# TensorE's branch around the rare paths, placed behind a product that waits for VectorE's last scaling

## The chip, the cores and the metric

The kernel runs on one core of a Trainium2 chip. The metric is the device time of one execution in microseconds (us). The kernel before takes 631.93 us, the median of three executions (631.75, 631.93 and 632.38).

## The reference, cut to what matters

Two branches over the same 2048 x 448 input are mixed with a gate for each token:

```
g = sigmoid((x * gate_w).sum(-1))
a = Cr @ (x @ Wr.T) - Ci @ (x @ Wi.T)            # Fourier mixing, real part
gates = softmax(x @ wg); top 2 of 8 experts, weights cw renormalised
h = gelu(einsum("nd,edf->nef", x, w1))            # 8 experts, 448 -> 1792
b = einsum("ne,ned->nd", cw, einsum("nef,efd->ned", h, w2))
return g * a + (1 - g) * b
```

The change touches none of these results.

## The kernel before, in words

The program has one straight part and one conditional part. The straight part computes the Fourier branch by the symmetries of the DFT matrices and the experts with a fixed capacity of rows for each (496 to 576). The conditional part, the rare paths, repeats work in a general way: tokens beyond an expert's capacity, and inputs whose DFT matrices lack the symmetries. VectorE finds out in the straight part whether either is needed and writes it into a small tile, `flags`. With these inputs neither is needed.

The expert work runs over `jobs`, pairs of an expert and one of its 14 blocks of 128 hidden columns. `up` makes a block's hidden values (the matmuls of line 777), `down` multiplies them by the second weight matrix (line 837) into one accumulator for each tile of up to 128 rows. The last four blocks of the last expert are multiplied together, in `down(*range(last - 3, last + 1))`, tile after tile. When a tile's products are complete, `combine` scales it by the tokens' weights (VectorE in lines 881 and 888, ScalarE in line 890), and `scatter` has GpSimd send its rows to `out` by an indirect DMA (line 900). The very last tile, 112 rows, is the one scaling of line 881; the rows that it adds to were fetched before (line 896), and its scatter is the last work of the straight part.

Then come two lines that all five engines execute:

```
    rest = nc.values_load(flags[0:1, 2:3], min_val=0, max_val=1)
    ctx.enter_context(tc.If(rest > 0))
```

Each engine loads the flag into a register (TENSOR_LOAD, line 1127), compares, and takes a branch over the code of the rare paths (COMPARE_BRANCH, shown under `_compat.py:109`) to the end of the program. There it sets right the semaphores that the skipped code would have changed (EVENT_SEMAPHORE, `_compat.py:109`), and all engines meet (line 1322): SyncE waits for the semaphores of every engine and of every DMA queue one after the other, each engine reports, and GpSimd clears the semaphores.

Each engine has its own sequence of instructions, written out in the order of the program (`tc.manual_schedule` for TensorE, VectorE, ScalarE and SyncE). TensorE's ends with the matmuls of line 837; nothing in its sequence waits for the scaling that follows them, so its TENSOR_LOAD and its branch stand directly behind its last matmul. The rows of an engine's sequencer are marked by a q (PEldq for TensorE's, DVEq, ACTq, POOLq, SPq). The engines' instructions themselves are brought from memory by DMAs, the rows of kind "instruction" among the DMA queues: q8 moves 16 KB a packet and q14 8 KB.

Of the kernel before, what the change touches and what calls it, by code (L numbers as in the profile page):

```python
# [9 lines left out]
F32 = mybir.dt.float32  # L10
# [9 lines left out]
P = 128  # L20
# [47 lines left out]
def tiles_of(cap):  # L68
    return [min(P, cap - c * P) for c in range((cap + P - 1) // P)]
# [3 lines left out]
def tile_kernel(ctx: ExitStack, tc: tile.TileContext, xt, xrows, xplain, wg, whid, cq, cw, cspec, edge, refs, wquad, whall, cgen, wcat, out):  # L73
    nc = tc.nc
    te, ve, se, gp, sp = nc.tensor, nc.vector, nc.scalar, nc.gpsimd, nc.sync

    keep = ctx.enter_context(tc.tile_pool(name="keep", bufs=1))
    rp = ctx.enter_context(tc.tile_pool(name="rp", bufs=1))
    stream = ctx.enter_context(tc.tile_pool(name="stream", bufs=3))
    ps = ctx.enter_context(tc.tile_pool(name="ps", bufs=3, space=bass.MemoryType.PSUM))  # L80
# [130 lines left out]
    def apart(e):  # L211
        return CAPS[e] - FULL * P == Q
# [601 lines left out]
    def down(*us, behind=None):  # L814
        e = jobs[us[0]][0]
        tl = tiles_of(CAPS[e])
        if jobs[us[0]][1] == 0:
            for c in range(len(tl)):
                Y[c] = psy.tile([P, 512], F32, name=f"y{BANKS[c]}")
        sent = []  # L820
        turns = [(c, u) for c in range(len(tl)) for u in us]
        if len(us) == 4:
            turns[3:5] = turns[4:2:-1]
        for c, u in turns:
            f, n = jobs[u][1], tl[c]
            if c == FULL and apart(e):
                few(e, u, sent)
                continue
            m = n if c < FULL else 2 * n
            cs = slice(c * P, c * P + m)  # L830
            wh, wl = (w[:, :D] for w in V[u])
            gh, gl = GH[u]
            steps = [(gh[:, cs], wh), (gh[:, cs], wl)]
            if c < FULL:
                steps.append((gl[:, cs], wh))
            for s, (a, b) in enumerate(steps):
                te.matmul(Y[c][:m, :D], a, b, start=f == 0 and s == 0, stop=f == NF - 1 and s == len(steps) - 1)  # L837
            if f == NF - 1:
                combine(e, c, n, sent)
                if behind and c == FULL - 2:  # L840
                    behind()
        for u in us:
            del W[u], V[u], GH[u]

    def few(e, u, sent):
        f = jobs[u][1]
        if f + 1 not in LOTS:
            return
        lot = range(u - f + max(b for b in LOTS if b <= f), u + 1)
        for i in range(0, len(lot), NQ):  # L850
            group = lot[i : i + NQ]
            wide = NQ // len(group)
            for j in range(NQ):
                v = group[j // wide]
                cs = slice(j % wide * (D // wide), (j % wide + 1) * (D // wide))
                te.matmul(Y[FULL][j * Q : (j + 1) * Q, cs], REST[v], RAW[v][1][:, cs], start=f < LOTS[1] and i == 0, stop=f == NF - 1 and i + NQ >= len(lot), tile_position=(0, j * Q))
        for v in lot:
            del RAW[v], REST[v]
        if f == NF - 1:
            rt["rear"] = Y[FULL], sent  # L860
# [16 lines left out]
    def combine(e, c, n, sent):  # L877
        wt = rt["wgt"][:n, e, c : c + 1]
        ys = mp.tile([P, D], F32, name="ys", bufs=NCT)
        if (e, c) == (E - 1, FULL - 1):  # L880
            ve.scalar_tensor_tensor(ys[:n], Y[c][:n, :D], wt, rt["base"][:n], op0=OP.mult, op1=OP.add)
        elif c == FULL:
            yt = mp.tile([P, D], F32, name="yt", bufs=1)
            ve.tensor_copy(yt[:n], Y[c][n : 2 * n, :D])
            ve.tensor_tensor(yt[:n], Y[c][:n, :D], yt[:n], OP.add)
            ve.tensor_scalar(ys[:n], yt[:n], wt, None, op0=OP.mult)
        elif c % 2 == 0:
            ve.tensor_scalar(ys[:n], Y[c][:n, :D], wt, None, op0=OP.mult)  # L888
        else:
            se.activation(ys[:n], Y[c][:n, :D], AF.Copy, scale=wt)  # L890
        scatter(e, c, n, ys, sent, None if (e, c) == (E - 1, FULL - 1) else OP.add)
# [177 lines left out]
    def side_work(s):  # L1069
        s -= SIDE  # L1070
        quad_dma(*divmod(s - 2, PACE))
        if s == 3:
            edges_dma()
        if s == 6:
            edges()
        q, r = divmod(s - 4, PACE)
        if 0 <= q < len(units):
            quad_check(q, r)
        e, f = divmod(s + SIDE, NF)
        if e > 1 and apart(e - 1) and f < 2:  # L1080
            rear(e - 1, f)
        if 1 <= e <= NQT and f in (2, NF - 1):
            blend(2 * (e - 1) + f // (NF - 1))
        if e == NQT + 1 and f == 3:
            blend_mid()
        end = 4 + PACE * len(units)
        if s == end:
            verdict()
        if s == end + 1:
            tell()  # L1090
        if len(summed) > len(mixed):
            send(*summed[len(mixed)])
            if len(mixed) == NT:
                tc.keep_in_program_order(gp.drain())
                ahead(E - 1, FULL - 1)
        if s > end + 1 and 1 <= f < (NF - 3 if e == E - 1 else NF - 1) and len(summed) < NT:
            mix(len(summed))

    up(UP, lambda: advance(2))
    for u in range(UP, last):  # L1100
# [19 lines left out]
        if not split:  # L1120
            side_work(u - UP)
    down(*range(last - 3, last + 1))
    order.close()
    late.close()

# [7 lines left out]
    with tc.For_i(0, n_ov) as j:  # L1133
# [31 lines left out]
        for f in range(NF):  # L1165
# [3 lines left out]
            acc = ps.tile([P, 512], F32, name="acc")  # L1169
# [18 lines left out]
    with tc.For_i(0, n_a) as j:  # L1188
# [3 lines left out]
        for h in range(2):  # L1192
            hf = full.tile([P, 2 * D], F32, name="hf")
            for u in range(2):
                acc = ps.tile([P, 512], F32, name="acc")
# [4 lines left out]
    with tc.For_i(0, n_b) as i:  # L1200
        acc = psy.tile([P, 512], F32, name="y0")
# [125 lines left out]
```

## Time and profile before

| | |
|---|---|
| median of three executions | 631.93 us |
| the profiled execution, its whole time | 632.4 us |
| its span, first to last instruction | 630.8 us |
| VectorE, ScalarE, GpSimd busy | 80%, 46%, 35% of the span |
| moved by DMA | 122.96 MB |
| instruction fetches on q8, on q14 | 30 and 33 packets |

The whole time is 1.6 us above the span. TensorE is in work through nearly all of the span; its granted clock is 0.998 of full speed. What the change touches lies in the last 8 us, where the engines finish one after the other, so the views to read are the instructions in order of time near the end, the rows of single source lines (they hold the sequencers' own instructions, which count as no engine's busy time), and the DMA queues in short windows. In the views of windows and of DMA queues a packet counts with its whole time where it starts.

### The profile page before, as it was taken

What the parts mean: (1) busy time and instruction counts of PE and PEld (TensorE: products, weight loads), DVE (VectorE), ACT (ScalarE), POOL (GpSimd) and SP (SyncE); (2) the same over time, 40 slices, a digit from 0 to 9 for tenths busy, and PEclk for the clock granted to TensorE, in tenths of its full rate; (3) what the DMA queues carried; (4) which work ended last, traced back from release to release, by engine and by line L of the source; (5) the groups of instructions that cost most, each with busy time, mean ns of one, the idle gap of its engine ahead of it and who ended that gap; (6) DMA issues with size and microseconds to landing.
All of it is one profiled execution on the core that took longest, in us unless ns stands there. A gap on an engine that the chain in (4) does not pass through costs nothing. (4 is left out here: it accounts for less than half of the span.)

```text
span 630.8 us, 10868 instructions
## 1 busy us (share of the span) xinstructions
PE 621.8 (99%) x3581; PEld 556.5 (88%) x3581; DVE 503.8 (80%) x1261; ACT 287.1 (46%) x588; POOL 217.7 (35%) x199
## 2 busy tenths in 40 slices
PE   9999999999999999999999999999999999999995
PEld 5999999989998999989999788888888888888884
DVE  7889797689977999779896799988997788666551
ACT  2543233365565565564664434333342334544440
POOL 2210084554254353344440444333241342142113
PEclk9999999999999999999999999999999999999999
DMA  8546454588777777786776867879566737768734
GB/s 344 181 158 212 163 178 140 162 184 289 227 235 193 203 241 230 226 192 205 245 233 218 196 189 240 259 200 286 177 219 193 153 120 150 157 156 162 154 70 60
DMA packets 58751, 122.96 MB, mean 195 GB/s; under 512 B 8305, under 2 KB 31921, under 8 KB 58689
## 3 DMA queue, kind: packets, MB, share of 16 engines
q1 hardware_dynamic: 47376, 101.95, 49.6%
q0 software_dynamic: 11168, 20.20, 17.9%
q8 instruction: 30, 0.49, 0.3%
q14 instruction: 33, 0.26, 0.1%
q10 hardware_dynamic: 144, 0.07, 0.0%
HBM read 106.09 MB, written 16.08 MB: 194 GB/s over the span
## 5 line engine op out<-in xcount | busy, mean ns | idle before, releaser
L777 PE MATMUL acc<-X,hi 128*128 128x288 f32 (+3 forms) x1050 | 216.5, 342 | 0.0
L667 POOL DMA_INDIRECT xg<-xrows,piece x115 | 127.5, 1109 | 208.3 <-DVE xq L676 132.0
L777 PEld LDWEIGHTS acc<-X,hi 128*128 128x128 f32 x1050 | 173.6, 188 | 19.5 <-issue 1.1
L837 PE MATMUL y<-dn,gh 128*128 128x448 f32 (+1 forms) x458 | 167.5, 366 | 0.0
L837 PE MATMUL y<-up,gh 128*128 128x448 f32 (+1 forms) x458 | 167.3, 365 | 0.0
L837 PE MATMUL y<-up,gl 128*128 128x448 f32 (+1 forms) x444 | 162.5, 366 | 0.0
L784 ACT ACTIVATE g<-acc 128x288 f32<-128x288 f32 (+3 forms) x126 | 61.4, 489 | 189.1 <-issue 117.6
L777 PE MATMUL acc<-X,lo 128*128 128x288 f32 (+3 forms) x672 | 134.6, 322 | 0.0
L777 PEld LDWEIGHTS acc<-X,lo 128*128 128x128 f32 x672 | 105.4, 188 | 10.3
L900 POOL DMA_INDIRECT out<-ys,tok x36 | 65.6, 1822 | 111.6 <-DVE ys L888 53.2
L837 PEld LDWEIGHTS y<-up,gh 128*128 128x128 f32 (+1 forms) x458 | 85.8, 187 | 7.6
L837 PEld LDWEIGHTS y<-dn,gh 128*128 128x128 f32 (+1 forms) x458 | 85.8, 187 | 7.3
L801 DVE TENSOR_TENSOR gl<-g,gh 128x512 fp32r<-128x512 f32 (+1 forms) x111 | 76.5, 689 | 18.5 <-ACT gh L795 11.0
L941 DVE CUSTOM_DVE_ANT_0 junk<-quads 128x512 f32<-128x512 f32 x128 | 88.0, 688 | 2.6 <-issue 0.3
L837 PEld LDWEIGHTS y<-up,gl 128*128 128x128 f32 (+1 forms) x444 | 83.2, 187 | 7.7 <-DVE gl L801 0.9
L223 DVE TENSOR_TENSOR lo<-raw,hi 128x512 fp32r<-128x512 f32 x112 | 77.1, 688 | 2.6 <-ACT hi L218 1.1
L797 DVE CAST gh<-g 128x512 fp32r<-128x512 f32 (+2 forms) x69 | 30.3, 439 | 54.8 <-ACT g L784 53.4
L218 ACT ACTIVATE hi<-raw 128x512 fp32r<-128x512 f32 x112 | 69.5, 620 | 0.0
L223 DVE TENSOR_TENSOR dn<-row,up 128x448 fp32r<-128x448 f32 x112 | 69.2, 618 | 0.0
L218 ACT ACTIVATE up<-row 128x448 fp32r<-128x448 f32 x112 | 63.3, 565 | 0.0
L784 ACT ACTIVATE g<-g 128x256 f32<-128x256 f32 x42 | 17.6, 418 | 46.3 <-DVE g L783 37.1
L782 ACT ACTIVATE g<-acc 128x256 f32<-128x256 f32 x42 | 15.9, 379 | 43.2 <-PE acc L777 31.7
(276 smaller groups left out, 433.4 us busy)
## 6 DMA issues: line engine op xcount, KB each, us to landing
quads<-cq SPq DMA_DIRECT2D x64, 512.0 KB
raw<-wcat SPq DMA_DIRECT2D x112, 256.0 KB
row<-wcat SPq DMA_DIRECT2D x112, 224.0 KB
out<-yt SPq DMA_DIRECT2D x21, 224.0 KB
xraw<-xt SPq DMA_DIRECT2D x8, 512.0 KB
out<-ot POOLq DMA_DIRECT2D x16, 224.0 KB
cw<-cw SPq DMA_DIRECT2D x4, 512.0 KB
xg<-xrows,piece POOLq DMA_INDIRECT x115
```

Of the source, the lines that this page charges most:

```text
L218: se.activation(hi[:, : raw.shape[-1]], raw, AF.Copy)
L223: ve.tensor_tensor(lo[:, :n], raw, r32(hi[:, :n]), OP.subtract)
L667: st = gp.indirect_dma_start(out=xg[:, q], out_offset=None, in_=xrows, in_offset=bass.IndirectOffsetOnAxis(ap=rt["piece"][:, e, g : g + 1] ...
L777: te.matmul(acc[:, :m], a, b, start=s == 0, stop=s == len(steps) - 1)
L782: se.activation(g[:, cs], acc[:, n : 2 * n], AF.Copy)
L784: se.activation(g[:, cs], g[:, cs] if both else acc[:, :n], AF.Gelu_apprx_tanh)
L797: ve.tensor_copy(gh[:, :top], g[:, :top])
L801: ve.tensor_tensor(gl[:, :main], g[:, :main], r32(gh[:, :main]), OP.subtract)
L837: te.matmul(Y[c][:m, :D], a, b, start=f == 0 and s == 0, stop=f == NF - 1 and s == len(steps) - 1)
L900: st = gp.indirect_dma_start(out=out, out_offset=bass.IndirectOffsetOnAxis(ap=rt["tok"][:n, e, c : c + 1], axis=0), in_=ys[:n], in_offset= ...
L941: ve.tensor_tensor_reduce(out=junk[:, :512], in0=row(a[0])[:, a[1] * 512 : a[1] * 512 + 512], in1=row(b[0])[:, b[1] * 512 : b[1] * 512 + 5 ...
```

## The change

Ahead of the flag's load, one value for each partition is set to zero by VectorE, and TensorE multiplies that column with itself into one element of an accumulator that nobody reads:

```diff
     down(*range(last - 3, last + 1))
+    done = keep.tile([P, 1], F32, name="done")
+    ve.memset(done, 0.0)
+    te.matmul(ps.tile([P, 512], F32, name="acc")[:1, :1], done, done, start=True, stop=True)
     order.close()
     late.close()
```

On VectorE the memset stands between the last scaling (line 881) and the flag's load:

```order
 L888 TENSOR_SCALAR ys<-y_6883,wgt 128x448
 L881 SCALAR_TENSOR_TENSOR ys<-y_6884,wgt,yt 112x448
-L1127 TENSOR_LOAD flags
+L1124 MEMSET done 128x1
+L1130 TENSOR_LOAD flags
 _compat.py:109 COMPARE_AND_BRANCH
```

The memset has no wait of its own; it follows the scaling in VectorE's order.

On TensorE, at the end of the straight part (y_6884 is the last tile's accumulator), the new product stands between the last matmul and the flag's load:

```order
 L837 MATMUL y_6884<-dn,hi 112x448
 L837 MATMUL y_6884<-up,lo 112x448
-L1127 TENSOR_LOAD flags
+L1125 MATMUL acc<-done 1x1
+L1130 TENSOR_LOAD flags
 _compat.py:109 COMPARE_AND_BRANCH
```

The product waits for a semaphore of VectorE, which the memset raises. The flag's load and the branch, which directly followed the last matmul, now follow the product. The sequences of ScalarE, GpSimd and SyncE are the same but for line numbers, three higher behind the change (1127 is 1130, 1322 is 1325).

`done` takes 4 bytes of each partition in the pool `keep`. Pools begin at multiples of 32 bytes, so those that are laid out behind `keep` from the same side (`rp`, `stream` with the weights, `hid`, `lp`, `xp` with the experts' inputs) begin 32 bytes later; the other pools stay where they were.

## The prediction

> **What bounds the kernel now.** I read the page first: who is busy through the span.
>
> ```profile
> span 630.8 us, 10868 instructions
> PE 621.8 (99%) x3581; PEld 556.5 (88%) x3581; DVE 503.8 (80%) x1261; ACT 287.1 (46%) x588; POOL 217.7 (35%) x199
> ```
>
> TensorE is in work for 621.8 of 630.8 us, and the change adds to its stream nothing before its last regular matmul. So only the tail can move. The second view is the instructions in order of time (start, duration) at the end.
>
> ```profile
> 618.43 0.64 ACT L890 ACTIVATE ys<-y,wgt 128x448 f32<-128x448 f32 x1 [4.23 <-PE y L837]
> ...
> 622.86 0.36 PE L837 MATMUL y<-up,lo 128*112 128x448 f32 x1
> 623.26 0.69 DVE L881 SCALAR_TENSOR_TENSOR ys<-y,wgt,yt 112x448 f32<-112x448 f32 x1 [1.72 <-PE y L837]
> 624.22 0.96 POOL L900 DMA_INDIRECT out<-ys,tok  x1 [0.85 <-DVE ys L881]
> ```
>
> Last matmul to 623.2, last scaling to 623.95, last scatter issued by 625.2; then 5.6 us in which no engine computes. What fills them stands in the sequencers' rows (duration in ns min/median/max, first and last start in us): the flag's loads of line 1127, the branches of `_compat.py:109`, the meeting of line 1322, and SyncE's waits.
>
> ```profile
> L1127 ACTq TENSOR_LOAD <-flags x1: 468/468/468, 618.4 to 618.4; - x1
> L1127 PEldq TENSOR_LOAD <-flags x1: 835/835/835, 619.5 to 619.5; - x1
> L1127 DVEq TENSOR_LOAD <-flags x1: 544/544/544, 623.3 to 623.3; - x1
> L1127 POOLq TENSOR_LOAD <-flags x1: 918/918/918, 624.0 to 624.0; - x1
> ```
>
> ```profile
> _compat.py:109 ACTq COMPARE_BRANCH x1: 45/45/45, 619.0 to 619.0; - x1
> _compat.py:109 PEldq COMPARE_BRANCH x1: 4982/4982/4982, 620.4 to 620.4; - x1
> _compat.py:109 DVEq COMPARE_BRANCH x1: 72/72/72, 623.9 to 623.9; - x1
> _compat.py:109 POOLq COMPARE_BRANCH x1: 57/57/57, 625.0 to 625.0; - x1
> ```
>
> ```profile
> L1322 SPq EVENT_SEMAPHORE x14: 17/28/28, 629.2 to 630.7; - x14
> ...
> L1322 SPq DRAIN x3: 7/7/13, 629.9 to 630.2; - x3
> ...
> L1322 PEldq DRAIN x2: 8/8/8, 625.7 to 630.3; - x2
> ```
>
> ```profile
> SPq L1322 <- DMA out<-ys,tok: 26.8, 1, 26.8
> ```
>
> The end hangs on the last scatter: SyncE waits for its landing until 629.2, and the fixed meeting takes the other 630.8 - 629.2 = 1.6 us. TensorE's branch is the odd row: 4.98 us (620.4 to 625.4) where the others need 0.05 to 0.07. It is off the path now: TensorE has reported at 625.7.
>
> Why does the scatter, issued by 625.2, land only at 629.2? The third view is the DMA queues in short windows (packets, MB, share of 16 engines' time). For 622.0 to 622.2, then for 621.9 to 624.2:
>
> ```profile
> q8 instruction: 1, 0.02, 60.7%
> ```
>
> ```profile
> q8 instruction: 1, 0.02, 5.3%
> ```
>
> One 16 KB fetch starts at about 622.1, 1.7 us into TensorE's branch, and takes 0.053 x 16 x 2.3 = 1.95 us, to 624.05; the branch ends 1.35 us later. So the branch waits for code. For 626.5 to 626.65, 626.5 to 631.0, and for 627.0 to 629.0 with its 40 slices of 0.05 us:
>
> ```profile
> q8 instruction: 1, 0.02, 59.8%
> ```
>
> ```profile
> q8 instruction: 1, 0.02, 2.0%
> ```
>
> ```profile
> DMA  0000000000000000000700000000000100000000
> ...
> q0 software_dynamic: 3, 0.01, 2.1%
> ```
>
> A second fetch starts at about 626.58, 1.2 us after the branch ended, and takes 0.020 x 16 x 4.5 = 1.44 us, to 628.0. Between 627 and 629 just three packets of the scatters start (q0), the first in the slice 627.95 to 628.0, as that fetch ends, the last two by 628.6. All others had started before 627.0:
>
> ```profile
> 626.00:626.50 0.50, 0.00 (x0) 0.00 (x0) 0.00 (x0) 0.00 (x0) 0.00 (x0) 1.00 0.72 215
> 626.50:627.00 0.50, 0.00 (x0) 0.00 (x0) 0.00 (x0) 0.00 (x0) 0.00 (x0) 1.00 0.44 132
> 627.00:627.50 0.50, 0.00 (x0) 0.00 (x0) 0.00 (x0) 0.00 (x0) 0.00 (x0) 1.00 0.00 0
> ```
>
> (The two numbers at a row's end are DMA share and GB/s.) I read: one of the 16 DMA engines held the end of the last scatter behind TensorE's second fetch. The last packet starts near 628.57 and the scatter has landed at 629.2, 0.6 us later. Without that fetch it would have landed at 627.3 to 627.6.
>
> **The change, part by part.**
>
> *The memset.* The same form elsewhere:
>
> ```profile
> L205 DVE MEMSET raw<- x2: 59/59/59, 37.9 to 37.9; 128x1 f32 x2
> ```
>
> 0.06 us behind the scaling's end at 623.95: 624.0. It delays VectorE's own flag load and branch by as much, and VectorE is done some 5 us before the end: nothing.
>
> *The product.* TensorE is idle from 623.2, so its work costs nothing. Its wait is the change: queued behind it on TensorE are the flag's load, the branch, and the two fetches. All move from 619.5 to 624.1 (GpSimd's flag load, released by the same scaling, starts at 624.0; its DMA at 624.22; so 624.0 to 624.2). No DMA of the kernel is moved and no queue passed.
>
> *The flag's load.* 0.835 us is TensorE's own; bounds 0.47 and 0.92 (ScalarE's, GpSimd's). The branch follows 0.1 us later (620.4 less 620.3). Branch start: 624.1 + 0.84 + 0.1 = 625.0 (624.6 to 625.2), instead of 620.4.
>
> *The branch.* At most 4.98 us as now. Below: request 1.2 (second fetch), transfer 1.0, tail 0.6 (as the scatter's landing) = 2.8. The transfer is the mean over all q8 packets, 0.003 x 16 x 630.8 / 30:
>
> ```profile
> q8 instruction: 30, 0.49, 0.3%
> ```
>
> I take request 1.4, between its two values; transfer 1.4, that of the second fetch, which met the same scatter; tail 1.0, between 0.6 and 1.35. Sum 3.8: the branch ends at 628.8 (627.4 to 630.2).
>
> *The end through TensorE.* Its reports follow 0.3 us behind the branch (625.4 to 625.7). SyncE passes its waits one after the other (14 rows), and which of them are TensorE's the row does not tell. From there to the end it is between 0.9 us (SyncE's drain at 629.9 to 630.8) and 1.6 us (the whole meeting); I take 1.2. Span by this path: 628.8 + 0.3 + 1.2 = **630.3** (628.6 to 631.7).
>
> *The end through the scatter.* The fetch that stood at 622.1 would start near 625.0 + 1.4 = 626.4, while the scatter still runs (share 0.72 and 0.44), and the second fetch would follow only behind the branch, after the landing. So the scatter meets one fetch again, or just misses it. Landing between 627.3 and 629.2; half of a 1.4 us transfer lost gives 628.2. Span: 628.2 + 1.6 = 629.8 (628.9 to 630.8).
>
> *The 32 bytes* by which weights and inputs move cost nothing that I can find. The nearest rows are two differences of line pairs 1047 and 1049, whose sources start one element apart and which take the same time:
>
> ```profile
> 600.82 0.39 DVE L1047 TENSOR_TENSOR ot<-fold 128x225 f32<-128x225 f32 x1
> 601.13 0.39 DVE L1049 TENSOR_TENSOR ot<-fold 128x224 f32<-128x224 f32 x1
> ```
>
> They speak for VectorE alone. For TensorE and the loads nothing is shown; 0.2% either way stays open.
>
> *Sum.* The later path is TensorE's: span 630.3, with the 632.4 - 630.8 = 1.6 us around it 631.9, which is 0.5 below the profiled execution's own 632.4. That execution is the highest of three, 0.45 over the median, and whether its excess lies in this tail cannot be told. If it does, the tail of the median execution has no 0.5 to give; if not, the time would be 631.4. I take the middle: **631.7**.
>
> **Where a page speaks against it.** On ScalarE the flag's load starts at 618.4, with the scaling of 618.43 that waited 4.23 us for TensorE; on VectorE at 623.3, with the scaling of 623.26. In both, what stands behind a waiting instruction waits too. On TensorE the load started at 619.5, 3.4 us ahead of the last matmul's start, so its sequencer runs far ahead of the array; but those matmuls waited for nothing. [...]
>
> **The rivals.**
>
> 1. *The branch does not move.* TensorE queues the waiting product and goes on to the branch at 620.4. Then both fetches stay and the time is that of now: 632.4 against the profiled execution, 631.9 against the median. For it: the 3.4 us lead. Against: the two engines' rows. 0.10.
>
> 2. *Both fetches miss the scatter and the branch is short.* The fetch starts at 626.7 or later, behind the scatter's last packets, or slips through; landing at 627.5, and a branch at its lower bounds ends by 627.6. Span 629.0 to 629.1, time 630.6, and 630.2 to 630.6 on the median's scale: faster by 0.2 to 0.3%. For it: with the first fetch gone from 622.1, no DMA engine starts the last scatter late. Against: the fetch is due at 626.2 to 626.9, the scatter's packets start until 627.0, and the branch would have to lose 2.2 of its 5 us. 0.15.
>
> 3. *The branch becomes the end, at full length: slower.* All of its 4.98 us is its own and not the traffic's. From 625.2 it ends at 630.2, and the span is 630.2 + 0.3 + 1.2 = 631.7, time 633.3: 0.9 over the profiled execution, 0.2% over the median. It decides from the point where the branch ends after 629.0, as then TensorE's report passes the landing of 629.2 less the waits ahead of it. For it: only one such branch is measured. Against: its fetch ran beside three scatters, and a mean fetch takes half of 1.95 us. 0.07, and 0.01 more that the 32 bytes cost time.
>
> **How the numbers follow.** Forecast 0.67, the three rivals 0.33 (0.10, 0.15, 0.08). About 0.2%, 1.26 us, is what a measurement of this kernel can tell from no change: below 630.67 is faster, above 633.19 slower. The forecast's own spread (630.7 to 632.9) lies inside, and so does rival 1: same 0.77. Faster 0.15, rival 2. Slower 0.08. The range reaches from rival 2's middle, 630.4, to 632.9, a little short of rival 3.
>
> **What would show it.** Right: TensorE's flag load starts at 624.0 to 624.2; its branch starts near 625.0 and lasts 3 to 4.5 us; no q8 packet starts between 614 and 626; SyncE's wait for the scatter ends before 629.0, and a wait for TensorE may take its place. Wrong: TensorE's load still at 619.5 (rival 1); a landing before 627.6 with a branch of under 3 us (rival 2); a branch of 5 us with the landing well before it (rival 3). A matmul or a load of weights that is longer by a constant share through the whole span would mean that the 32 bytes count, and that the tail was the wrong place to look.

## The result, and the profile after

The changed kernel takes 638.58 us (median of five, 638.05 to 638.78) against 631.87 us before (631.55 to 632.38): a ratio of 1.0104, 95% interval 1.0089 to 1.0119. It is slower by 6.7 us, and its time lies far above the predicted range, which ended at 632.9.

The tail did about what was forecast. In order of time, at the end of the changed kernel:

```profile
628.79 0.37 PE L837 MATMUL y<-up,lo 128*112 128x448 f32 x1
629.20 0.68 DVE L881 SCALAR_TENSOR_TENSOR ys<-y,wgt,yt 112x448 f32<-112x448 f32 x1 [1.76 <-PE y L837]
629.83 0.06 DVE L1124 MEMSET done<- 128x1 f32 x1
629.96 0.09 PEld L1125 LDWEIGHTS acc<-done 128*1 128x1 f32 x2 [1.19 <-DVE done L1124]
629.96 0.19 PE L1125 MATMUL acc<-done 128*1 128x1 f32 x2 [0.80 <-DVE done L1124]
630.16 0.96 POOL L900 DMA_INDIRECT out<-ys,tok  x1 [0.89 <-DVE done L1124]
```

TensorE's flag load and branch, SyncE's final meeting and its wait, in the rows of their source lines and of SyncE's waits:

```profile
L1130 PEldq TENSOR_LOAD <-flags x1: 826/826/826, 630.0 to 630.0; - x1
```

```profile
_compat.py:109 PEldq COMPARE_BRANCH  x1: 4418/4418/4418, 630.9 to 630.9; - x1
```

```profile
L1325 SPq EVENT_SEMAPHORE  x14: 17/28/28, 635.3 to 636.8; - x14
```

```profile
SPq L1325 <- DMA out<-ys,tok: 27.0, 1, 27.0
```

And the DMA queues from 631.9 to 634.0, then from 633.2 to 636.0 (with its 40 slices of 0.07 us) and from 635.5 to 637.0:

```profile
q0 software_dynamic: 56, 0.16, 24.3%
q8 instruction: 1, 0.02, 5.5%
```

```profile
DMA  0000000000500000002000000000000000000000
...
q0 software_dynamic: 4, 0.01, 2.0%
```

```profile
q8 instruction: 1, 0.02, 4.0%
```

The load waits for the product and the branch moves with it. The branch's fetch now falls on the last scatter. It takes 0.055 x 16 x 2.1 = 1.85 us, by its record in the trace from 632.09 to 633.93. The scatter's last four packets start only from 633.9 on, as the fetch ends. The second fetch comes behind the landing. SyncE waits for the scatter until 635.3. From the last matmul's start to the end of the span it was 630.8 - 622.86 = 7.94 us; now it is 636.9 - 628.79 = 8.11 us. The tail has cost 0.2 us. The other 5.9 us of the 6.1 by which these two profiled executions differ had been lost before the last matmul started.

Two long stretches show where. Before, from 140 to 340 us and from 360 to 560 us (busy us and count of instructions for each engine; the first pair is TensorE's matmuls):

```profile
140.00:340.00 200.00, 200.00 (x1232) 184.03 (x1231) 175.37 (x455) 117.30 (x255) 79.82 (x60) 1.00 0.75 227
360.00:560.00 200.00, 200.00 (x933) 174.54 (x932) 168.32 (x406) 79.49 (x148) 64.53 (x57) 1.00 0.68 192
```

After:

```profile
140.00:340.00 200.00, 200.00 (x1221) 182.52 (x1220) 173.05 (x448) 117.44 (x251) 77.22 (x60) 1.00 0.73 219
360.00:560.00 200.00, 200.00 (x918) 172.00 (x918) 167.23 (x403) 77.24 (x145) 63.77 (x56) 1.00 0.68 191
```

TensorE is busy without a gap in this view and at full clock (the 1.00 near the row's end) in both, yet it gets through 0.9% and 1.6% fewer matmuls. The groups by shape (count, busy us, mean ns of one), before and after:

```profile
L837 PE MATMUL y<-up,gh 128*128 128x448 f32 x445 | 162.6, 365 | 0.0
...
L777 PE MATMUL acc<-X,hi 128*128 128x288 f32 x476 | 74.2, 295 | 0.0
...
L777 PE MATMUL acc<-X,lo 128*128 128x512 f32 x168 | 44.9, 389 | 0.0
```

```profile
L837 PE MATMUL y<-up,gh 128*128 128x448 f32 x445 | 164.0, 368 | 0.0
...
L777 PE MATMUL acc<-X,hi 128*128 128x288 f32 x476 | 74.3, 295 | 0.0
...
L777 PE MATMUL acc<-X,lo 128*128 128x512 f32 x168 | 45.6, 393 | 0.0
```

Matmuls overlap (those of line 837 last 365 or 366 ns in the groups of before and start 203.0 ns apart), so what counts is the spacing, the time from one's start to the next one's. It is worked out here from the starts in the traces, over all pairs that follow each other in the same line; gaps to other lines and waits (gaps over 260 ns) are left out, and 512 columns means here those read in one piece (two pieces of 256 are left out). The mean spacing of the 448-column products of line 837 went from 203.0 to 206.2 ns, that of 512 columns in line 777 from 228.1 to 230.8 and that of 496 columns from 220.3 to 224.0. The mean of 288 columns, with all their gaps, stayed at 132.4 to 132.7.

Summed over every gap from one matmul's start to the next, line 837 grew by 3.5 us, line 777 by 2.3 and the rest by 0.1: the whole 5.9 us ahead of the tail. (The step of 3.2 ns times all 1372 products of line 837 would be 4.4 us. But line 837's gaps to other lines did not grow, and the profiled execution before had five longer gaps in line 837, of 271 to 392 ns, that the changed one did not have; they are 0.6 us over the others.)

### The profile page after: what moved, and what is told of

Its sections match the earlier page's. It is cut to its first block, busy times and chain, and to the rows that moved or that the text cites. A ratio compares the mean times of both kernels' runs of the same rounds, so it can differ in the third digit from the quotient of the medians.

```text
span 636.9 us, 10873 instructions
## 1 busy us (share of the span) xinstructions
PE 628.0 (99%) x3583; PEld 557.2 (87%) x3583; DVE 505.1 (79%) x1262; ACT 289.7 (45%) x588; POOL 214.1 (34%) x199
## 5 line engine op out<-in xcount | busy, mean ns | idle before, releaser
L667 POOL DMA_INDIRECT xg<-xrows,piece x115 | 125.9, 1095 | 214.4 <-DVE xq L676 129.1
L900 POOL DMA_INDIRECT out<-ys,tok x36 | 63.5, 1765 | 113.3 <-DVE ys L888 55.3
L1063 POOL DMA_DIRECT2D out<-ot x16 | 13.9, 870 | 59.8 <-ACT ot L1062 50.1
## 6 DMA issues: line engine op xcount, KB each, us to landing
row<-wcat SPq DMA_DIRECT2D x112, 224.0 KB, 3.5
out<-yt SPq DMA_DIRECT2D x21, 224.0 KB, 3.2
out<-ot POOLq DMA_DIRECT2D x16, 224.0 KB, 3.9
```

What stands on the lines that cost most here:

```text
L667: st = gp.indirect_dma_start(out=xg[:, q], out_offset=None, in_=xrows, in_offset=bass.IndirectOffsetOnAxis(ap=rt["piece"][:, e, g : g + 1] ...
L900: st = gp.indirect_dma_start(out=out, out_offset=bass.IndirectOffsetOnAxis(ap=rt["tok"][:n, e, c : c + 1], axis=0), in_=ys[:n], in_offset= ...
L1063: st = gp.dma_start(out[i * P : (i + 1) * P, :], ot[:, :D], accum_op=OP.add)
```

## The experiments

The change had two sides: the product's wait, and 4 bytes in `keep`, by which the weights' and inputs' pools moved 32 bytes. The theories are these: **A**, the addresses slow the matmuls; **B**, the wait costs the time somewhere. All ratios are to the kernel before on the same chip. The edits of e1 to e3 are shown against the changed kernel, those of e4 to e12 and of e16 against the kernel before.

**e1_old_tile**: the change without a tile of its own.

```diff
-    done = keep.tile([P, 1], F32, name="done")
-    ve.memset(done, 0.0)
-    te.matmul(ps.tile([P, 512], F32, name="acc")[:1, :1], done, done, start=True, stop=True)
+    ve.memset(quad, 0.0)
+    te.matmul(ps.tile([P, 512], F32, name="acc")[:1, :1], quad, quad, start=True, stop=True)
```

> The wait alone: VectorE sets an existing column (quad, unused in this program) to zero and TensorE multiplies that, so no tile is added and every address is that of before. Theory A (the 32 bytes by which the weights and inputs moved slow the matmuls): the line 837 matmuls follow each other every 203 ns as before, the time is 631.0 to 632.6, and only the tail differs. Theory B (the product's wait costs the 6.7 us somewhere): 637 to 639.

632.20 us, ratio 1.000 (0.999 to 1.001), spacing in line 837 203.1 ns. The wait costs nothing and brings nothing: B falls. SyncE's waits in this run:

```profile
SPq L1324 <- DMA out<-ys,tok: 26.4, 1, 26.4
...
SPq L1324 <- PEq _compat.py:109: 0.2, 1, 0.2
```

SyncE waits for the scatter's landing until 628.8 us in this run, and then 0.2 us more for TensorE's branch, which lasts from 624.9 to 629.0:

```profile
_compat.py:109 PEldq COMPARE_BRANCH  x1: 4098/4098/4098, 624.9 to 624.9; - x1
```

**e2_tile_only**: the tile without the product.

```diff
-    te.matmul(ps.tile([P, 512], F32, name="acc")[:1, :1], done, done, start=True, stop=True)
```

> The tile alone: 4 bytes more in the pool keep and the memset, no product, so TensorE branches behind its last matmul as before. Theory A: 637.5 to 639, line 837 matmuls every 206 ns. Theory B: 631.5 to 632.4.

638.51 us, ratio 1.0096 (1.0076 to 1.0116), spacing 206.1 ns. The 32 bytes alone make the whole loss. Its group of line 837 stands as in the changed kernel:

```profile
L837 PE MATMUL y<-up,gh 128*128 128x448 f32 x445 | 163.9, 368 | 0.0
```

**e3_64_bytes**: the change with a tile of 64 bytes.

```diff
-    done = keep.tile([P, 1], F32, name="done")
+    done = keep.tile([P, 16], F32, name="done")[:, :1]
```

> The whole change with a tile of 64 bytes for each partition instead of 4, so the pools behind keep move by 64 bytes. Theory A with a period of 64 bytes: 631.0 to 632.6 and 203 ns. Theory A with any longer period (128 or 256 bytes), or a cost of any move at all: 637 or more. Theory B: 637 to 639.

628.81 us, ratio 0.9947 (0.9928 to 0.9967): neither of the expected values, but faster than before. Line 837 is at 200.2 ns. So it is no cost of leaving an old place, and what 64 bytes did was no return to the pace of before.

Next, the operands one by one. A matmul has two: a loaded one (128 x 128, the LDWEIGHTS rows of PEld, 187 ns each in line 837) and a streamed one (the columns of the MATMUL rows, 448 in line 837). In line 837 the loaded one is gh or gl, the streamed one up or dn, the two parts of the second weight matrix; in line 777 the loaded one is hi or lo and the streamed one X.

**e4_down_32**, **e5_down_64**, **e6_down_128**, **e12_down_16**: the layout of before; up and dn are used OFF = 8, 16, 32 or 4 columns inside their tiles of 512.

```diff
         V[k] = [stream.tile([P, DX], F32R, name=n, bufs=4) for n in ("up", "dn")]
+        V[k] = [t[:, OFF:] for t in V[k]]
```

> The kernel before with every pool where it was; only the second weight matrix, as split into its two parts (up, dn), is written and read 8 columns (32 bytes) further inside its own tiles. It is the streamed operand of the line 837 matmuls and of no other. Theory A, by the streamed operand's address: 837 goes from 203 to 206 ns, 1400 of them by 3.1 ns give 4.3 us, 636.2; line 777 stays at 227 ns for 512 columns. If the loaded operand, the DMA writes or the pools' places count instead: 631.5 to 632.4.

> As e4_down_32, but 16 columns (64 bytes) instead of 8; all else as before. The streamed operand of the line 837 matmuls starts at 64 past a multiple of 256, the loaded operand where it was. If the streamed operand's own address sets the pace: 837 goes from 203.0 to 200.2 ns as in e3_64_bytes, 1372 of them by 2.8 ns give 3.8 us less, 628.5, and line 777 is unchanged. If e3_64_bytes was faster for another reason (place of the raw weights, of the pools): 631.5 to 632.8.

> As e5_down_64, but 32 columns (128 bytes). If the pace repeats every 128 bytes: 203.0 ns and 632.4, as before. If it repeats every 256 bytes or more, or if only the distance to the loaded operand counts and 64 was the right side of it: another value, 200 to 206 ns, 628 to 637.

> As e4_down_32, but 4 columns (16 bytes). If anything off a multiple of 64 bytes costs one more 64-byte line: as 32 bytes, 205 to 206 ns, 635 to 636.5. If the grain is 32 bytes and 32 itself is the bad place: between 203 and 206, or worse than 206 if 16 bytes leave a 32-byte grain as well.

Ratios 1.0052 (1.0032 to 1.0072), 0.9957 (0.9940 to 0.9973), 1.0006 (0.9996 to 1.0016) and 1.0020 (1.0009 to 1.0030); spacing in line 837 205.1, 200.8, 203.8 and 203.0 ns. One offset of the streamed operand of one line costs 3.3 us or saves 2.4. In the groups of e4_down_32, then e5_down_64 (their edit makes line 837 line 839):

```profile
L839 PE MATMUL y<-up,gh 128*128 128x448 f32 x445 | 163.5, 367 | 0.0
```

```profile
L839 PE MATMUL y<-up,gh 128*128 128x448 f32 x445 | 161.3, 362 | 0.0
```

e12_down_16 tells two guesses apart, and both lose: 16 bytes are no multiple of 64 and cost line 837 nothing. Its 0.2% stands in line 777, whose 512 columns went to 231.5 ns although no address of that line had moved.

**e7_x_32**, **e10_x_64**: only X moves, XO = 8 or 16 columns, in tiles that are 16 or 32 columns larger.

```diff
+    def inputs():
+        n = (2 * NC - 1) * CMAX
+        t = xp.tile([P, n + 16], F32R, name="X")[:, XO : XO + n]
+        return t.rearrange("p (c n) -> p c n", n=CMAX)
...
-            X[e] = xp.tile([P, 2 * NC - 1, CMAX], F32R, name="X")
+            X[e] = inputs()
```

> The kernel before, only the experts' inputs X, the streamed operand of the line 777 matmuls, stand 32 bytes further inside a tile that is 64 bytes larger. If the streamed operand's address counts in line 777 too: 512 columns go from 227.8 to 231 ns, 496 from 220.3 to 224, 288 stay within 1; some 530 matmuls by 3.3 ns and 126 paired ones by 1 give 1.8 us, 634.2. If the loaded operand's 32 bytes were what slowed line 777 in the changed kernel: 632.4 and 227 ns.

> The kernel before, only X, the streamed operand of line 777, stands 64 bytes further inside tiles that are 128 bytes larger; its weights stay at multiples of 512. Theory D: line 777 gains as 837 did, 512 columns from 228 to 225 ns and 288 by 1 to 2 ns; 540 by 3 and 970 by 1.5 give 3 us, 628.5 to 630. If 64 apart does nothing in line 777 (or costs 3 ns at 496 columns as in e3_64_bytes): 631.5 to 633.

635.65 us, ratio 1.0061 (1.0045 to 1.0078), and 635.30 us, 1.0048 (1.0033 to 1.0064). The edit of e7_x_32 puts the buffers of X 32 or 96 bytes from the loaded operand, since the wider tiles shift every second one. In e7_x_32 512 columns are at 233.5 ns and 496 at 225.5, in e10_x_64 at 231.5 and 226.6. So X counts too, but 64 bytes apart, good for line 837, are bad for line 777. A group of e7_x_32 (line 777 is line 783 there):

```profile
L783 PE MATMUL acc<-X,lo 128*128 128x512 f32 x168 | 45.9, 395 | 0.0
```

**e8_loaded_32**: e2_tile_only with both streamed operands moved on by 32 bytes (the edits of e4 and e7), so that only the loaded operand of line 777 stays off a multiple of 64.

> The kernel with the tile alone (all pools 32 bytes further, as in e2_tile_only), with both streamed operands (up and dn; X) written and read 32 bytes further inside their tiles, so that they start at multiples of 64 again, while the loaded operand of line 777 (hi, lo), the raw weights, the gathered rows and the routing tiles stay 32 bytes off. If only streamed operands count: like e3_64_bytes, 628.5 to 630, line 837 near 200 ns, line 777 without its 3 to 4 ns. If the loaded operand or the DMAs' destinations count: line 777 stays at 231 ns, or the time stays above 632.

632.62 us, ratio 1.0012 (1.0002 to 1.0021). Line 837 is at 200.3 ns as expected, but line 777 at 233.4 and 224.9 ns, as in e7_x_32, though X stood at multiples of 64: the loaded operand's place counts there as well. The rule "the streamed operand's address alone" falls.

**e9_loaded_64**: the loaded operand of line 837 moves by 64 bytes.

```diff
-            gh = mp.tile([P, CMAX + RMAX], F32R, name="gh", bufs=3)
-            gl = mp.tile([P, FULL * P], F32R, name="gl", bufs=3)
+            gh = mp.tile([P, CMAX + RMAX + 32], F32R, name="gh", bufs=3)[:, 16:]
+            gl = mp.tile([P, FULL * P + 32], F32R, name="gl", bufs=3)[:, 16:]
```

> The kernel before, only the loaded operand of the line 837 matmuls (gh, gl, the hidden values) stands 64 bytes further inside tiles that are 128 bytes larger; the streamed operand is where it was. Theory D (what counts is where the streamed and the loaded operand start against each other, modulo 128 bytes: 64 apart is best, 0 or 128 apart costs 3 ns, 32 apart 6 ns): 837 goes from 203.0 to about 200.5 ns, 628.4 to 629.8. Theory S (the streamed operand's own address alone): 203 ns, 631.5 to 632.5.

632.53 us, ratio 1.0003 (0.9994 to 1.0013), line 837 at 202.8 ns. Theory D, in the form that 64 apart is 64 apart on either side, falls too. (512 columns in line 777 went to 229.8 ns here, with both their operands where they were.)

**e11_both_64**: e5_down_64 and e10_x_64 together.

> up, dn and X all 64 bytes further (e5_down_64 and e10_x_64 together), no other change and none of the original one. If the two add up: the 2.4 us of e5_down_64 and whatever e10_x_64 shows, 626 to 629.5. If line 777 does not gain: 629 to 630.

630.83 us, ratio 0.9976 (0.9965 to 0.9986): above the upper end of what was expected. Line 837 kept its gain (200.5 ns), line 777 its loss (230.5 and 225.7).

**e13_grid** and **e14_grid_busy**: the cost by itself. The computation is left out and zeros are written; TensorE runs rows of 20 matmuls (on zeros) from two streamed and two loaded tiles, and in the second VectorE and ScalarE work beside it.

```diff
+LOADED = (0, 8, 16, 24)
+STREAMED = (0, 4, 8, 12, 16, 20, 24, 28, 32)
...
+    for n in (448, 512):
+        for w in LOADED:
+            for s in STREAMED:
+                for k in range(20):
+                    te.matmul(acc[:, :n], loads[k % 2][:, w : w + P], streams[k % 2][:, s : s + n], start=True, stop=True)
+                if BUSY:
+                    for k in range(7):
+                        ve.tensor_tensor(side[0], side[1], side[1], OP.subtract)
+                        se.activation(side[2], side[3], AF.Copy)
```

> Leaves the whole computation out and writes zeros: rows of 20 float32r matmuls from two streamed and two loaded tiles, nothing else running. 448 and 512 columns, streamed operand 0 to 128 bytes past a multiple of 256 in steps of 16, loaded operand 0, 32, 64 or 96 bytes past. If the streamed operand's address itself sets the pace: spacings of 203, 206 and 200 ns at 0, 32 and 64 bytes, repeated at 128. If address only counts together with other traffic (theory T: TensorE's reads meet VectorE's, ScalarE's and the DMAs' in the SBUF): the same spacing in all 72 rows, within 0.5 ns, and below 203 at 448 columns.

> As e13_grid (the computation left out, zeros written), with VectorE and ScalarE kept at work on tiles of their own beside it (differences and copies of 512 columns, 7 of each for a row of 20 matmuls). If address alone counts: as e13_grid. Theory T: spacings rise above those of e13_grid and differ by some ns between the addresses.

In e13_grid nothing but the matmuls and the writing of zeros ran; the whole time was 328.1 us, in e14_grid_busy 373.2. The mean spacings of the 72 rows differ between the two by 0.05 ns at most: it is no contention with VectorE or ScalarE. (One gap of 391 ns at the very start is left out.) Here are nine of the fifteen distances of the streamed from the loaded operand's start, in bytes, for the loaded operand at 0, 32, 64 and 96 (a dash: not run), in ns:

| distance | 448 columns | 512 columns |
|---|---|---|
| -64 | - / - / 201.9 / 202.1 | - / - / 233.4 / 232.9 |
| -32 | - / 203.5 / 204.4 / 204.5 | - / 233.4 / 233.2 / 233.2 |
| -16 | - / 203.1 / 202.7 / 202.4 | - / 235.9 / 227.1 / 227.1 |
| 0 | 206.3 / 203.0 / 202.6 / 202.6 | 227.7 / 226.8 / 228.7 / 228.7 |
| 16 | 201.9 / 200.2 / 203.1 / 203.1 | 231.4 / 231.4 / 231.4 / 231.4 |
| 32 | 200.1 / 204.5 / 206.1 / 206.1 | 233.5 / 233.5 / 233.5 / 233.5 |
| 64 | 199.9 / 200.3 / 200.1 / - | 229.4 / 229.4 / 229.4 / - |
| 96 | 205.2 / 205.2 / - / - | 233.9 / 233.9 / - / - |
| 128 | 203.7 / - / - / - | 232.8 / - / - / - |

In most rows the distance sets the spacing: 512 columns at 32 apart take 233.5 ns from all four places, at 64 apart 229.4, and 448 columns at 64 apart 199.9 to 200.3. Sides count: 64 and -64 are different (448 columns take 199.9 to 200.3 and 201.9 to 202.1 ns). The two lengths want different distances, 64 for 448 columns (199.9 to 200.3 ns), 0 for 512 (226.8 to 228.7). Some cells break the rule: 448 columns at 0, 16 and 32, and 512 at -16 and 0. One break is at the very distance of the change, where 448 columns take 200.1 ns in one row and 204.5 to 206.1 in the three others. Whether the place of the operands or the row's past does that, the grid does not tell. Theory T falls, since the spacings differ with nothing beside the matmuls; the distance, with its sign, is theory D2, and it is a rule with exceptions.

**e15_after_down_8**: the changed kernel, product and wait included, with the one edit of e4_down_32. It brings line 837 from 32 to 64 bytes apart.

> The changed kernel with one part of its layout altered: up and dn are used 8 columns (32 bytes) inside their tiles, so the line 837 matmuls have their streamed operand 64 bytes past the loaded one's place modulo 128 instead of 32. All else, the product's wait too, is the changed kernel's. Theory D2 (spacing goes by the distance between streamed and loaded operand, as in e13_grid): 837 falls from 206.2 to 200.3 ns, 1372 by 5.9 ns give 8.1 us less than 638.6, 630.5; line 777 keeps the changed kernel's 230.8 and 224 ns. If the 32 bytes cost elsewhere than in 837 in the main: 634 or more.

630.23 us, ratio 0.9974 (0.9964 to 0.9983), line 837 at 200.2 ns, against the changed kernel's 638.58 in the measurement of the result. In place of the loss there is a gain over the kernel before. Line 777, at the changed kernel's addresses, was at 229.1 and 223.4 ns instead of 230.8 and 224.0: it gave back a little without having been touched.

```profile
L839 PE MATMUL y<-up,gh 128*128 128x448 f32 x445 | 160.8, 361 | 0.0
```

**e16_64_bytes_only**: e3_64_bytes without the product.

```diff
+    done = keep.tile([P, 16], F32, name="done")
+    ve.memset(done, 0.0)
```

> A tile of 64 bytes in keep, set to zero at the end and not used: no product and no wait, and the pools behind keep move by 64 bytes as in e3_64_bytes. If that run's gain is the layout alone: 628.3 to 629.3, within 0.5 us of e3_64_bytes, line 837 near 200.3 ns. If the product's wait had a part in it: nearer to 630.5.

628.33 us (627.63 to 628.63), ratio 0.9943 (0.9929 to 0.9956): the layout alone, and faster than both kernels. In the two stretches from above:

```profile
140.00:340.00 200.00, 200.00 (x1235) 185.03 (x1234) 175.08 (x455) 119.27 (x256) 78.81 (x60) 1.00 0.74 222
360.00:560.00 200.00, 199.98 (x941) 175.97 (x940) 169.19 (x405) 81.08 (x151) 67.69 (x59) 1.00 0.68 191
```

941 matmuls in the second stretch, against 933 before and 918 in the changed kernel.

All runs of the whole kernel beside each other; distance is that of the streamed from the loaded operand in bytes, by the tiles' addresses and without whole multiples of 128 but for e6 (a dozen of line 837's 1372 products, those of the last hidden block, lie otherwise in the runs whose pools moved and in e9):

| run | 837: distance | 448 columns | 777: distance | 512 | 496 | ratio |
|---|---|---|---|---|---|---|
| before | 0 | 203.0 | 0 | 228.1 | 220.3 | 1 |
| changed | 32 | 206.2 | 0 | 230.8 | 224.0 | 1.0104 |
| e1 | 0 | 203.1 | 0 | 228.1 | 220.3 | 1.000 |
| e2 | 32 | 206.1 | 0 | 230.8 | 224.0 | 1.0096 |
| e3 | 64 | 200.2 | 0 | 227.1 | 223.3 | 0.9947 |
| e4 | 32 | 205.1 | 0 | 229.2 | 220.3 | 1.0052 |
| e5 | 64 | 200.8 | 0 | 229.1 | 223.4 | 0.9957 |
| e6 | 128 | 203.8 | 0 | 226.8 | 221.1 | 1.0006 |
| e7 | 0 | 203.1 | 32, 96 | 233.5 | 225.5 | 1.0061 |
| e8 | 64 | 200.3 | 32, 96 | 233.4 | 224.9 | 1.0012 |
| e9 | -64 | 202.8 | 0 | 229.8 | 221.7 | 1.0003 |
| e10 | 0 | 203.3 | 64 | 231.5 | 226.6 | 1.0048 |
| e11 | 64 | 200.5 | 64 | 230.5 | 225.7 | 0.9976 |
| e12 | 16 | 203.0 | 0 | 231.5 | 220.6 | 1.0020 |
| e15 | 64 | 200.2 | 0 | 229.1 | 223.4 | 0.9974 |
| e16 | 64 | 200.2 | 0 | 227.1 | 223.3 | 0.9943 |

In line 837 the distance orders the runs: 202.8 to 203.8 ns at 0, 128, 16 and -64, 205.1 to 206.2 at 32, 200.2 to 200.8 at 64. In line 777 it does not suffice: at a distance of 0 the 512 columns take 226.8 to 231.5 ns.

## Why the prediction was wrong, point by point

**The step that failed** is the one on the 32 bytes: "cost nothing that I can find", with "0.2% either way" left open and a chance of 0.01 in rival 3. They cost 0.96% by themselves (e2_tile_only), more than half of it by the spacing of line 837's products, 206.1 ns instead of 203.0. The rows quoted for it were VectorE's, and VectorE was not what the time hung on. The page showed TensorE busy for 99% of the span, so whatever touches its operands counts about 1400 times (line 837) and 1700 times (line 777) over; the prediction found that the change "adds to its stream nothing" and took that for a stream in which nothing changes. The distance in line 837 went from 0 to 32 because its two operands lie in pools on different sides: `stream` moved, `mp` with gh and gl did not. The prediction did name the sign to look for, a matmul longer by a constant share through the whole span. That is what the profile after shows for 448, 496 and 512 columns.

**Right, in the tail:**

- The product holds TensorE's sequencer. Its flag load starts at 630.0, 0.1 us behind the end of the last scaling (629.88); rival 1, by which TensorE would go on to the branch past the waiting product, falls.
- The branch starts at 630.9, 1.0 us behind the scaling's end, as worked out (625.0 after 623.95). It lasts 4.42 us where 3.8 was taken, inside the bounds of 2.8 and 4.98. By the fetch's record its parts are: request 1.2 us (1.4 taken), transfer 1.85 (1.4), tail 1.4 (1.0).
- No q8 packet starts in the tail before 632, and the scatter meets the branch's own fetch in place of the second one. Its landing is 635.3 - 629.9 = 5.4 us behind the scaling's end, where it was 629.2 - 623.95 = 5.2 before; the forecast 628.2 would have been 4.2. In e1_old_tile it was 4.9 (628.8, the scaling's end at 623.9). Half a transfer was too little: the last packets waited for the end of the fetch (633.9), as before (628.0).
- With the layout restored (e1_old_tile) the span is 630.5 us, where the sum gave 630.3, and the ratio is 1.000. As forecast, the wait for the scatter ends before 629.0 there and TensorE's branch comes last (4.10 us, to 629.0). Rivals 2 and 3 did not occur in that run. The part of the change that the prediction was about moves the time by nothing that can be measured. The branch was 0.3 us longer there than summed and began 0.1 us earlier; in the changed kernel it was 0.6 us longer, so that the spans agree within 0.2 us is in part luck.

**Two slips in the sum.** The upper end of the span through TensorE, 631.7, takes 1.2 us from the report to the end, though the bound stated for it is 1.6 (632.1). The forecast's own spread begins at 630.7, though the lower bound of the later path, 628.9, gives 630.5 or less. Neither changes the forecast. And the sum went half-way because the excess of 0.45 us of the profiled execution might lie in its tail; the five longer gaps in line 837, 0.6 us near 127, 132 and 457 us, are another place for it.

**What stays open.** Line 777 in the changed kernel kept its distance of 0, since both its operands moved by 32 bytes, and yet its 512 columns went from 228.1 to 230.8 ns. In e12_down_16, e6_down_128 and e9_loaded_64 they took 231.5, 226.8 and 229.8 ns with every address of their own unchanged, and in e5_down_64 the 496 columns went to 223.4. The traces show more than these means. Products of 512 columns read in one piece stand 11 in a row, in 40 of 42 rows directly behind line 837. Here are the ten spacings within a row, by place, as means of the 42 rows in ns (gaps of over 300 ns left out):

| run | 837: distance | 1 | 2 | 3 | 4 | 5 | 6 | 7 | 8 | 9 | 10 |
|---|---|---|---|---|---|---|---|---|---|---|---|
| before | 0 | 230.6 | 232.3 | 231.1 | 226.8 | 227.1 | 227.0 | 226.6 | 226.8 | 226.7 | 226.5 |
| e5 | 64 | 230.7 | 235.5 | 228.5 | 232.4 | 230.7 | 226.8 | 226.6 | 226.7 | 226.6 | 226.8 |
| e4 | 32 | 230.1 | 224.5 | 230.9 | 235.6 | 228.0 | 232.5 | 230.4 | 226.7 | 227.1 | 226.4 |
| changed | 32 | 230.0 | 233.3 | 235.6 | 224.6 | 230.6 | 235.9 | 228.4 | 232.4 | 230.9 | 226.5 |
| e12 | 16 | 234.3 | 230.8 | 233.4 | 235.3 | 224.4 | 231.0 | 235.1 | 228.3 | 232.3 | 230.5 |

After one to three spacings the last four rows run through parts of one series (235, 224, 231, 235, 228, 232, 231) towards a rest near 226.6, and the kernel before is at rest from the fourth place. e4, e5 and e12 changed the operand of line 837 alone. So the matmuls ahead of line 777 set where in the series it starts, and in these rows the changed kernel loses by a late rest. That holds for 512 columns only: the 496 columns of the changed kernel go round in four spacings (221, 223, 227 and 222 ns) and come to no such rest. What sets the starting point was not found. Nor was why the distance counts, and why 64 is good for 448 columns and not for 512.

## What to carry to other kernels

Where an engine is busy through the whole span, a change that adds no work to it can still change the pace of its instructions (here a tile of 4 bytes took the spacing of line 837 from 203.0 to 206.1 ns, e2_tile_only): look at what a new tile, however small, does to the addresses of the pools laid out behind it. Before a change is judged, its layout should be taken apart from its work, by running the tile alone and the work on an old tile. On such a kernel, try a pad ahead of a pool, or an offset in the streamed tile, in several sizes: here a tile of 64 bytes was worth 0.57% (e16_64_bytes_only) for two lines. Measure it on the whole kernel, since the same 64 bytes in X cost 0.48% (e10_x_64).

## What the runs showed of the hardware that was not expected

- The spacing of float32r matmuls depends in most rows on how far apart the streamed and the loaded operand start: 199.9 to 206.6 ns for 448 columns and 226.8 to 235.9 ns for 512 in the grid, 3 to 4% between the extremes, with TensorE alone at work. VectorE and ScalarE beside it changed it by 0.05 ns at most.
- It depends on the matmuls before as well: with its own operands where they were, a row of 512 columns in line 777 took 226.8 to 231.5 ns on average, by the place of line 837's operands alone (e6_down_128, e12_down_16).
- 288 columns hardly react: 132.4 ns before, 132.7 changed, and 133.1 with X 32 or 96 bytes apart (e7_x_32).
- A taken branch on TensorE took 3.86 to 4.98 us in the sixteen kernels (e6_down_128 the shortest, the kernel before the longest), each with a fetch of 16 KB of code within it, where the other engines' took 0.05 to 0.07. The last of a scatter's packets started only as such a fetch ended (628.0 us before, 633.9 changed).
